# A hint for one branch, given to four engines at the head of the program

## The chip, the cores and the metric

The kernel runs on one core of one Trainium2 chip. The metric is the device time of one execution in microseconds, from start to end on the chip, as the median over several runs. Five engines work from instruction streams of their own: TensorE (PE in the profile, with PEld for its weight loads), VectorE (DVE), ScalarE (ACT), GpSimd (POOL) and SyncE (SP), which here only starts DMAs and waits for semaphores. A q behind an engine's name (SPq) stands for its sequencer.

## What is computed

Three parts follow each other, in float32 on inputs of which some are stored as float64:

```python
# attention: batch 4, 8 heads, 768 steps, head size 48
for t in range(S):
    state = alpha[:, :, t, :, None] * state + einsum('bhd,bhe->bhde', k[:, :, t], v[:, :, t])
    y[:, :, t] = einsum('bhd,bhde->bhe', q[:, :, t], state)
# first feed-forward part: xk, xr mix each row of x with the row before it
k = maximum(xk @ w_k, 0.0)
x = 1 / (1 + exp(-(xr @ w_r))) * (k * k @ w_v)
# second: a convolution over three rows as a gate
h = maximum(x @ w_in, 0.0)
out = (h * sigmoid(conv3(h, conv_w))) @ w_out
```

## The kernel before, in words

The attention's recurrence is computed in chunks of 128 steps (24 in all) with matrix products, which is exact enough only while alpha stays between 0.75 and 1.25 and the float64 words stay in range. The feed-forward parts run on tiles of 256 rows, with each float32 factor split into a high and a low part, so that three matmuls stand for one. All of this is recorded first as a list of operations (`pl`), which a planner (`Plan`) puts into an order for each engine from its own table of costs; `pl.issue` (line 1096) then issues them. The change does not touch the planner or its input.

While it works, the kernel collects in a tile `odd` by how much any input is out of range. `in_range` (line 993) counts at the end in how many of the 128 partitions all is in range, through one DVE reduction, one small matmul and a cast into `odd_i`. Line 1097 loads that count from SBUF into a register of every engine (`values_load`, TENSOR_LOAD in the trace). Line 1098 then branches: with a count below 128, `step_by_step` (line 976) computes everything again in the slow way, step by step, in loops. With the inputs here the count is 128, so every engine jumps over that part, which is long in the programs of SP, PE, DVE and ACT. Behind the jump stand the instructions that bring the semaphores to the same values on both paths (they carry line 1098 in the trace: eight on SP, one on each of the others), and the end of the program, in which SP waits for all queues and engines, and all engines meet (line 1126, the launch).

```python
        n_even = nc.values_load(odd_i, min_val=0, max_val=P)
    with tc.If(n_even < P):
        step_by_step()
```

Of the kernel before, what the change touches and what calls it, by code (L numbers as in the profile page):

```python
# [442 lines left out]
def gated_scan_ffn_kernel(  # L443
# [20 lines left out]
    P = 128  # L464
# [63 lines left out]
    odd = cp.tile([P, NCH + 40], F32, name="odd")  # L528
# [56 lines left out]
    def narrow(dst, words, col=None):  # L585
        h, l = words[..., 1], words[..., 0]
        bits = dst.bitcast(I32)
        pl.vector.tensor_scalar(even(bits), even(h), 3, 0x3FFFFFFF, op0=ALU.logical_shift_left, op1=ALU.bitwise_and)
        pl.vector.scalar_tensor_tensor(bits, h, -0x40000000, bits, op0=ALU.bitwise_and, op1=ALU.bitwise_or)
        pl.vector.scalar_tensor_tensor(bits, l, 29, bits, op0=ALU.logical_shift_right, op1=ALU.bitwise_or)  # L590
        h = h.bitcast(F32)
        pl.scalar.activation(h, h, AF.Abs)
        if col is None:
            pl.vector.scalar_tensor_tensor(dst, h, least, dst, op0=ALU.is_ge, op1=ALU.mult)
        else:
            pl.scalar.activation(h, h, AF.Relu, scale=-1.0, bias=least_s, accum_out=odd[:, col:col + 1])

    def pieces(w):

        nr = ND if w.shape[0] == DM else 2  # L600
        n = RAW // nr
        return [(slice(r, r + nr), slice(c, min(c + n, w.shape[1])))
                for c in range(0, w.shape[1], n) for r in range(0, w.shape[0] // P, nr)]

    def weight(w, hi, lo, at, src, col, whole=None):
        r, c = at
        nr, n = r.stop - r.start, c.stop - c.start
        words = src.take(pl, I32)[:, 0:2 * nr * n]
        pl.sync.dma_start(words.rearrange("p (r n) -> p r n", r=nr),
                          w[r.start * P:r.stop * P, c].bitcast(I32).rearrange("(r p) n -> p r n", p=P))  # L610
        x = whole[:, r, c] if whole else cols(v2(temps.take(pl))[:, 0:nr * n], n)
        narrow(x, words.rearrange("p (r n t) -> p r n t", r=nr, t=2), col)
        if not whole:
            split(hi[:, r, c], lo[:, r, c], x)
# [148 lines left out]
    def advance(c):  # L763
        qc, vc = qd[c % 2], vt[c % 2]
        ps = [cols(scs.take(pl)[:, 0:ND * HC], HC) for _ in range(2)]


        work, last = [[] for _ in range(4)], [[] for _ in range(4)]
        for dt in range(ND):
            for quad in range(4):  # L770
                p, i = divmod(dt * 4 + quad, 3)
                for j in range(2):
                    h = slice(HC * j, HC * j + HC)
                    for hp in range(max(0, i - 1), min(2, i + 1)):
                        work[quad].append((j, dt, vc[h, p, 32 * (i + hp):32 * (i + hp) + 32], am[h, p, hp, :]))
                    if j or not first(c):
                        last[quad].append((j, dt, ub[j][:, p, 32 * i:32 * i + 32], qc[:, p, h]))
        order = [(quad, *w[n]) for lists in (work, last) for n in range(max(map(len, lists)))
                 for quad, w in enumerate(lists) if n < len(w)]


        start = {x[:2]: n for n, x in reversed(list(enumerate(order)))}
        stop = {x[:2]: n for n, x in enumerate(order)}
        with pl.group():
            for n, (quad, h, dt, x, y) in enumerate(order):
                pl.tensor.matmul(ps[h][32 * quad:32 * quad + 32, dt, :], x, y,
                                 start=n == start[quad, h], stop=n == stop[quad, h])
        j = c % 2
        if j == 0:
            if first(c):  # L790
                pl.gpsimd.memset(xt[:, :, 0:1], 0.0)
            else:
                pl.scalar.activation(xt[:, :, 0:1], xt[:, :, T:T + 1], AF.Copy)
        for h in range(2):
            t0 = 1 + C * j + HC * h
            pl.scalar.activation(xt[:, :, t0:t0 + HC], ps[h], AF.Copy)
# [204 lines left out]
    with tc.manual_schedule():  # L1001
        nc.vector.memset(ones, 1.0)
        make_identity(nc, ident)
        for y, eng in (((sa, sk, sq), nc.vector), *((x, pl.gpsimd) for x in early.values())):
            for x, fill in zip(y, (1.0, 0.0, 0.0)):
                eng.memset(cols(v2(x), 64)[:, 0:H, D:], fill)
        nc.vector.memset(ad, 0.0)
        nc.vector.memset(odd, 0.0)
        for x in kks.pool.tiles:
            nc.vector.memset(x[:, 0:NP * D], 0.0)  # L1010
        nc.vector.memset(least_s, least)
        nc.scalar.activation(odd1, ones[:, 0:1], AF.Sigmoid)
        for x in vt:
            nc.gpsimd.memset(x[:, :, D:80], 0.0)
        nc.gpsimd.memset(one_l, 0.0)
        nc.gpsimd.memset(v3(one_l)[:, :, C - 1:C], 1.0)
        nc.gpsimd.memset(rec_f, 0.0)
        mf = tmps.tiles[0]
        make_upper_triangular(nc, mf[:, :P])
        for i in range(2):  # L1020
            h = slice(HC * i, HC * i + HC)
            nc.vector.tensor_copy(mask[h], mf[h, h])
        for x in (am, *ub):
            nc.gpsimd.memset(x, 0.0)

        cw_raw = cp.tile([P, 3, NF, 2], I32, name="cw_raw")
        prep(0)
        col = NCH
        lent = Line(Pool([v2(ht)[:, 0:2 * RAW].bitcast(I32)]))
        for x, whole in zip(weights, (None, wrw, wvw, None, None)):  # L1030
            for y in pieces(x[0]):
                i = col - NCH
                weight(*x, y, lent if i < NLENT and i % 3 == 2 else raws, col, whole)
                col += 1
        for r in lent.roots:
            pl.seen.setdefault(ht.tensor.name, []).extend((True, 0, 4, -1, o) for o in r.ops)
        for x, y, z in ((mu_ks, nu_ks, mu_k), (mu_rs, nu_rs, mu_r)):
            pl.sync.dma_start(x, z.rearrange("(a p) -> p a", p=P))
            pl.vector.tensor_scalar(y, x, -1.0, 1.0, op0=ALU.mult, op1=ALU.add)
        for i in range(3):  # L1040
            pl.sync.dma_start(cw_raw[:, i], conv_w[i].bitcast(I32).rearrange("(f p t) -> p f t", p=P, t=2))
        narrow(cw, cw_raw)

        prep(1)

        def att(n):

            attend(n)
            advance(n)
            if n + 2 < NCH:  # L1050
                prep(n + 2)

        def early_k():
            return stage_k(mix(mu_ks, nu_ks, True), True), stage_r(mix(mu_rs, nu_rs, False, True))

        att(0)
        att(1)
        y = early_k()
        att(2)
        att(3)  # L1060
        x0 = stage_v(*y, True)
        y = early_k()
        settle(*weights[1], wrw)
        att(4)
        x1 = stage_v(*y, True)
        settle(*weights[2], wvw)
        big = stage_h(0, x0)
        att(5)
        stage_o(0, big, 0, True)
        xk = mix(mu_ks, nu_ks)  # L1070
        big = stage_h(1, x1)
        xr = mix(mu_rs, nu_rs)
        stage_o(1, big, 0, True)
        for u in range(2, NU):
            c0 = 2 * u + 2
            more = u + 1 < NU
            big = stage_k(xk)
            g = stage_r(xr)
            if more:
                attend(c0)  # L1080
            x = stage_v(big, g)
            if more:
                advance(c0)
                if c0 + 2 < NCH:
                    prep(c0 + 2)
            big = stage_h(u, x)
            if more:
                att(c0 + 1)
                xk = mix(mu_ks, nu_ks)
                xr = mix(mu_rs, nu_rs)  # L1090
            else:
                stage_last(T * NU - 1)
            stage_o(u, big)
        in_range()
        warm = lambda x: nc.tensor.matmul(x[0:64, 0:64], ones, ones, start=True, stop=True)
        pl.issue(600.0, 6, banks.pool, 30e3, warm)
        n_even = nc.values_load(odd_i, min_val=0, max_val=P)
    with tc.If(n_even < P):
        step_by_step()


# [31 lines left out]
```

## Time and profile before

| what | value |
|---|---|
| median of 3 runs | 591.57 us (589.94 to 591.70) |
| the profiled execution | 591.75 us, of which the span of its instructions is 590.0 us |
| PE busy | 561.5 us, 95% of the span |
| DVE, ACT, POOL busy | 497.2, 434.6, 13.3 us |
| last matmul issued for the output | near 579.8 us into the span |
| last write of the output started | 580.7 us |

All times in the profile count from the span's first instruction. Register, branch and semaphore instructions are not counted as busy, so the last 9 us of the span look empty in the views of busy time; the view of one source line shows them, with the time at which each started (to 0.1 us). Instructions reach an engine by DMA as well: queue q8 and queue q14 carry packets of kind "instruction".

### The profile page before, as it was taken

Reading aid. Unit: us, or ns where it says so; the run is one execution under the profiler, and the core shown is the slowest. Engines: PE = TensorE matmul, PEld = TensorE weight load, DVE = VectorE, ACT = ScalarE, POOL = GpSimd, SP = SyncE. Lnnn points to the kernel's source line nnn. Section 1 sums busy time; section 2 is a strip of 40 time slices with the busy share of each in tenths; the row PEclk is TensorE's granted clock in tenths of the full one; section 3 lists DMA queues with packets and bytes.
Section 4 is the critical chain, followed back from the end, with each engine's and each line's share of the span. In section 5 each row is a group of like instructions: output and inputs, shape, how many; then the busy total and the mean of one; then the engine's idle time right before and its main releaser. Section 6 shows DMA issues by size and latency. Waiting matters only on the chain.

```text
span 590.0 us, 18574 instructions
## 1 busy us (share of the span) xinstructions
PE 561.5 (95%) x7762; PEld 527.0 (89%) x7762; DVE 497.2 (84%) x1044; ACT 434.6 (74%) x1035; POOL 13.3 (2%) x61
## 2 busy tenths in 40 slices
PE   8689899999899999999999999999999999999993
PEld 7578788999789999998999999999999999999982
DVE  8998999999999989789789789789789788376280
ACT  3799998997669577677678677677678677587370
POOL 3000000000000000000000000000000000000000
PEclk9789999999979999999999999999999999999997
DMA  9988946003433323223223223223223111000000
GB/s 182 235 168 240 233 147 186 16 28 102 107 81 83 84 65 90 52 65 92 50 65 91 59 58 92 50 64 92 50 65 91 27 41 42 1 2 29 0 2 33
DMA packets 87408, 48.02 MB, mean 81 GB/s; under 512 B 49170, under 2 KB 81810, under 8 KB 87314
## 3 DMA queue, kind: packets, MB, share of 16 engines
q1 hardware_dynamic: 87314, 46.74, 32.4%
q8 instruction: 62, 1.02, 0.7%
q14 instruction: 32, 0.26, 0.1%
HBM read 42.00 MB, written 4.72 MB: 79 GB/s over the span
## 4 chain that ended last, share of the span: by engine, by line
PE 59%; DVE 26%; ACT 9%; issue 2%; DMA 1%; SPq 1%; POOL 1%; DVEq 0%; POOLq 0%; ACTq 0%
PE pf L297 49%; DVE tmp L297 8%; PE sc L297 7%; DVE x L297 4%; DVE qd L297 3%; PE kk L297 3%; ACT tmp L297 3%; DVE gt L297 2%; DVE bigl L297 2%; ACT raw L297 1%; ACT ht L297 1%; DMA sa<-in_alpha_dram 1%; DVE kd L297 1%; ACT bigh L297 1%; DVE bt L297 1%
## 5 line engine op out<-in xcount | busy, mean ns | idle before, releaser
L297 PE MATMUL pf<-bigh,wv 128*128 128x256 f32 x336 | 88.9, 308 | 1.6 <-DVE kd L297 1.6
L297 DVE SCALAR_TENSOR_TENSOR tmp<-ht,cw,tmp 128x256 f32<-128x256 f32 x192 | 86.3, 477 | 4.7 <-ACT tmp L297 4.2
L297 ACT ACTIVATE tmp<-tmp 128x256 f32<-128x256 f32 (+1 forms) x144 | 69.2, 485 | 25.4 <-DVE tmp L297 11.6
L297 PE MATMUL pf<-xh,wih 128*128 128x256 f32 x288 | 82.0, 286 | 2.6 <-ACT xh L297 1.5
L297 PE MATMUL pf<-xl,wih 128*128 128x256 f32 x288 | 81.2, 282 | 1.4 <-DVE xl L297 1.4
L297 PE MATMUL pf<-xl,wkh 128*128 128x256 f32 x288 | 81.0, 283 | 0.5 <-DVE xl L297 0.5
L297 PE MATMUL pf<-xh,wkh 128*128 128x256 f32 x288 | 79.1, 281 | 1.9 <-ACT xh L297 1.6
L297 PE MATMUL pf<-xh,wil 128*128 128x256 f32 x288 | 80.8, 281 | 0.0
L297 PE MATMUL pf<-xh,wkl 128*128 128x256 f32 x288 | 80.0, 280 | 0.0
L297 PE MATMUL pf<-bigh,wvh 128*128 128x256 f32 x240 | 68.3, 285 | 0.3 <-DVE bigl L297 0.3
L297 PE MATMUL pf<-bigl,wvh 128*128 128x256 f32 x240 | 66.8, 278 | 0.0
L297 PEld LDWEIGHTS pf<-bigh,wv 128*128 128x128 f32 x336 | 62.8, 188 | 4.4 <-DVE kd L297 2.0
L297 PE MATMUL pf<-woh,bigh 128*128 128x384 f32 x192 | 66.4, 347 | 0.1
L297 PE MATMUL pf<-woh,bigl 128*128 128x384 f32 x192 | 64.7, 345 | 0.0
L297 PE MATMUL pf<-wol,bigh 128*128 128x384 f32 x192 | 64.4, 339 | 0.0
L297 ACT ACTIVATE pf<-pf 128x512 f32<-128x512 f32 x88 | 51.1, 583 | 11.6 <-PE pf L297 10.1
L297 PEld LDWEIGHTS pf<-xh,wih 128*128 128x128 f32 x288 | 55.3, 192 | 3.9 <-ACT xh L297 1.8
L297 PEld LDWEIGHTS pf<-xl,wih 128*128 128x128 f32 x288 | 55.3, 192 | 1.9 <-DVE xl L297 1.9
L297 PEld LDWEIGHTS pf<-xh,wkh 128*128 128x128 f32 x288 | 54.3, 190 | 2.5 <-ACT xh L297 2.1
L297 PEld LDWEIGHTS pf<-xl,wkh 128*128 128x128 f32 x288 | 54.9, 191 | 1.3 <-DVE xl L297 0.9
L297 PEld LDWEIGHTS pf<-xh,wil 128*128 128x128 f32 x288 | 55.3, 192 | 0.0
L297 PEld LDWEIGHTS pf<-xh,wkl 128*128 128x128 f32 x288 | 55.1, 191 | 0.0
(164 smaller groups left out, 1393.3 us busy)
## 6 DMA issues: line engine op xcount, KB each, us to landing
vt<-in_v_dram SPq DMA_DIRECT2D x48, 96.0 KB, 3.1
out_dram<-ot SPq DMA_DIRECT2D x23, 192.0 KB, 2.0
sa<-in_alpha_dram SPq DMA_DIRECT2D x38, 96.0 KB, 2.2
sk<-in_k_dram SPq DMA_DIRECT2D x38, 96.0 KB, 2.4
sq<-in_q_dram SPq DMA_DIRECT2D x38, 96.0 KB, 2.3
raw<-in_moe_w_out_dram SPq DMA_DIRECT2D x4, 768.0 KB, 4.4
sa<-in_alpha_dram SPq DMA_DIRECT2D x38, 80.0 KB, 2.2
sk<-in_k_dram SPq DMA_DIRECT2D x38, 80.0 KB, 2.6
```

Of the source, the lines that this page charges most:

```text
L297: getattr(getattr(self.nc, x.eng), fn)(*args, **kw)
```

## The change

Two lines: the `If` gets a label, and a hint that the branch with that label is likely to be taken is asked for on PE, SP, DVE and ACT. POOL gets none.

```diff
         pl.issue(600.0, 6, banks.pool, 30e3, warm)
+
+        tc.mark_branch_hint_location("odd", "LikelyTaken", [getattr(mybir.EngineType, e) for e in ("PE", "SP", "DVE", "Activation")])
         n_even = nc.values_load(odd_i, min_val=0, max_val=P)
-    with tc.If(n_even < P):
+    with tc.If(n_even < P, label="odd"):
         step_by_step()
```

The call stands behind `pl.issue`, yet the hint lands at the head of each of the four programs. Here is SP's program against the one before, at its head and at the branch (tiles: `sa`, `sk` are loads of alpha and k, `ot` the rows of the output, `raw` a weight of the step-by-step path; ISA stands for register work and a range check on the loaded count).

```order
@@ -1,3 +1,4 @@
-L1126 UNCONDITIONAL_BRANCH
+L1128 UNCONDITIONAL_BRANCH
+L1128 BRANCH_PREFETCH_HINT
 L297 DMA sa<-in_alpha_dram 128x8x48
 L297 DMA sk<-in_k_dram 128x8x48
@@ -208,7 +209,7 @@
 L297 DMA out_dram<-ot_84 128x384
 L297 DMA out_dram<-ot_83 128x384
-L1097 TENSOR_LOAD odd_i
-L1097 ISA x2
-L1098 COMPARE_AND_BRANCH
+L1099 TENSOR_LOAD odd_i
+L1099 ISA x2
+L1100 COMPARE_AND_BRANCH
```

One instruction is added ahead of SP's first DMA; at the branch nothing is added or moved, only the line numbers differ by two. ACT's program shows the same at its head (`odd` and `ones` are small tiles):

```order
@@ -1,3 +1,4 @@
-L1126 UNCONDITIONAL_BRANCH
+L1128 UNCONDITIONAL_BRANCH
+L1128 BRANCH_PREFETCH_HINT
 L1012 ACT_TABLE_LOAD
 L1012 ACTIVATE odd_102<-ones 128x1
```

DVE and PE get the same one row each, POOL none. The built programs differ in one more thing that the diff does not name: the label to which line 1098 jumps is now marked to begin a block of instruction fetch, on all five engines. In the program before it has no such mark, while the heads of the loops inside `step_by_step`, whose closing branches carry hints already, do have it.

## Rows read from the trace of the kernel before

**Rows 1.** The page's head, and busy us by engine (share of the span).
```profile
span 590.0 us, 18574 instructions
PE 561.5 (95%) x7762; PEld 527.0 (89%) x7762; DVE 497.2 (84%) x1044; ACT 434.6 (74%) x1035; POOL 13.3 (2%) x61
```

**Rows 2.** Busy time by stretch, 580 to 590 us: PE, PEld, DVE, ACT, POOL, clock, DMA, GB/s.
```profile
580.00:581.00 1.00, 0.22 (x3) 0.09 (x2) 0.14 (x1) 0.49 (x1) 0.00 (x0) 1.00 0.53 192
581.00:582.00 1.00, 0.00 (x0) 0.00 (x0) 0.00 (x0) 0.00 (x0) 0.00 (x0) 1.00 0.48 172
...
584.00:585.00 1.00, 0.00 (x0) 0.00 (x0) 0.00 (x0) 0.00 (x0) 0.00 (x0) 0.50 0.00 0
...
589.00:590.00 1.00, 0.00 (x0) 0.00 (x0) 0.00 (x0) 0.00 (x0) 0.00 (x0) 0.50 0.00 0
```

**Rows 3.** Source line 1098, all engines: duration ns min/median/max, first and last start us.
```profile
L1098 SPq EVENT_SEMAPHORE  x8: 17/17/17, 585.5 to 588.6; - x8
L1098 ACTq COMPARE_BRANCH  x1: 50/50/50, 581.0 to 581.0; - x1
L1098 POOLq COMPARE_BRANCH  x1: 45/45/45, 581.1 to 581.1; - x1
L1098 DVEq COMPARE_BRANCH  x1: 72/72/72, 581.1 to 581.1; - x1
L1098 PEldq COMPARE_BRANCH  x1: 3548/3548/3548, 581.1 to 581.1; - x1
L1098 POOLq EVENT_SEMAPHORE  x1: 17/17/17, 581.5 to 581.5; - x1
L1098 SPq COMPARE_BRANCH  x1: 45/45/45, 581.9 to 581.9; - x1
L1098 PEldq EVENT_SEMAPHORE  x1: 51/51/51, 584.7 to 584.7; - x1
L1098 ACTq EVENT_SEMAPHORE  x1: 17/17/17, 585.0 to 585.0; - x1
L1098 DVEq EVENT_SEMAPHORE  x1: 21/21/21, 585.3 to 585.3; - x1
```

**Rows 4.** Waits of SP's queue: waited for, us in total, times, longest.
```profile
SPq L1098 <- SPq L1098: 6.1, 2, 3.6
```

**Rows 5.** Source line 1098 on SP, 584 to 587 us, then 587 to 589 us.
```profile
L1098 SPq EVENT_SEMAPHORE  x2: 17/17/17, 585.5 to 585.6; - x2
...
L1098 SPq EVENT_SEMAPHORE  x6: 17/17/17, 588.2 to 588.6; - x6
```

**Rows 6.** DMA by queue, 582.6 to 583.4 us, then 586.0 to 586.8 us.
```profile
DMA packets 1, 0.01 MB, mean 10 GB/s; under 512 B 0, under 2 KB 0, under 8 KB 0
...
q14 instruction: 1, 0.01, 4.1%
...
q14 instruction: 1, 0.01, 2.4%
```

**Rows 7.** The last write: SP's timeline from 580 us; DMA issues, 580 to 590 us.
```profile
580.70 0.33 SPq L297 DMA_DIRECT2D out_dram<-ot  x1
...
out_dram<-ot SPq DMA_DIRECT2D x1, 192.0 KB, 2.3
```

**Rows 8.** Source line 1126, the end of the program, on SP and on DVE.
```profile
L1126 SPq EVENT_SEMAPHORE  x10: 17/28/28, 588.7 to 589.9; - x10
...
L1126 DVEq DRAIN  x2: 10/14/17, 585.4 to 589.5; - x2
```

**Rows 9.** Source line 1115, the program's first instructions, on SP.
```profile
L1115 SPq MOVE  x4: 29/34/42, 0.0 to 0.2; - x4
```

**Rows 10.** DMA by queue, 0 to 14 us, then 14 to 26 us.
```profile
DMA packets 9624, 2.53 MB, mean 181 GB/s; under 512 B 9240, under 2 KB 9240, under 8 KB 9624
q1 hardware_dynamic: 9624, 2.53, 113.5%
...
q8 instruction: 3, 0.05, 1.9%
```

**Rows 11.** Busy time by stretch at the head, columns as in rows 2.
```profile
14.00:28.00 14.00, 8.53 (x243) 6.92 (x243) 13.04 (x26) 9.37 (x19) 0.00 (x0) 0.82 1.03 223
```

## The prediction

> **What bounds the kernel now.** Over the span as a whole PE does: it is busy for 95% of 590.0 us [rows 1]. The hint gives PE no less to multiply, so I looked for a stretch in which PE is not the limit and a branch is. The busy time by stretch shows it at once: the last engine work falls between 580 and 581 us, and from there to 590.0 us no engine is busy at all [rows 2]. These last 9 us hold only loads of the count, branches and semaphores, which that view does not count, so the next view is that of the branch's own source line [rows 3]. Read it per engine, from COMPARE_BRANCH to the EVENT_SEMAPHORE behind the jump. POOL: 581.1 to 581.5, 0.4 us. PE: the branch itself is recorded with 3548 ns. ACT: 581.0 to 585.0, 4.0 us. DVE: 581.1 to 585.3, 4.2 us. SP, which branches last because it had a write to start first: 581.9 to 585.5, 3.6 us. All five take the same jump; only POOL, whose program over the skipped path is short, arrives without a stall.
>
> SP then stalls a second time. Of its eight instructions behind the jump, two run at 585.5 and 585.6, and the other six from 588.2 to 588.6 [rows 5]. The list of SP's waits has both gaps in one row: 6.1 us in 2 waits, the longest 3.6, so the other is 2.5 [rows 4]. It names no engine and no data that SP waited for. What does move in these gaps is instructions: during the first, one packet of the instruction queue q14 between 582.6 and 583.4 us; during the second, one between 586.0 and 586.8 us [rows 6]. I read the first gap as the fetch of the block that holds the jump's target, and the second as the fetch of the next block, which is needed two instructions later because the target stands two short of a block's end. Everything behind is SP's: it starts its last waits at 588.7 us [rows 8], while DVE, the last of the others, had been through at 585.4 us [rows 8]. So **SP's two fetch stalls set the end.**
>
> The Trainium skill, in "Runtime: NRT & Kernel Launch", section "Instruction fetch mechanics", says that a jump to a target outside of the blocks that an engine holds must wait for a DMA of that block; the rows above agree, with 3.6 to 4.2 us on the three engines whose gap can be read.
>
> **The change, part by part.**
>
> *The hint instructions.* One each on SP, DVE, ACT and PE, at the head. No trace here has one. From below it costs nothing, where the engine waits for data anyway; from above I take SP's register moves, 29 to 42 ns [rows 9], and the longest of the branches without a fetch in it, 72 ns [rows 3]. SP's loads and DVE's first fills stand right behind it, so I count 0.05 us on the path, with ends 0 and 0.1.
>
> *The first stall.* If the block of the target is there when SP branches, the jump costs what POOL's does, 0.4 us, instead of 3.6: SP arrives at 582.3 us rather than 585.5, a gain of 3.2 us. From below the hint may save nothing (the block is not there), from above the whole 3.6. I take POOL's, the same instruction at the same place.
>
> *The second stall.* The mark that the label has now asks that the target begin a block. Then SP's eight instructions and the end of its program would stand in one block, and the 2.5 us wait falls away. No trace here shows what becomes of such a mark, so its worth lies between 0 and 2.5 us. I take 2.5: the target is two instructions short of the border, so little needs to be moved, and the mark is what the program's other hinted targets carry.
>
> *What is late next.* SP's third instruction behind the jump waits for the queue that carries the last write of the output. That write is issued at 580.7 us and lands 2.3 us later, at 583.0 us [rows 7]. SP would be there at 582.5 us (582.3 and two instructions, 0.1 us apart as in [rows 5]), so it now waits some 0.5 us for the write. From that third instruction to the end it takes 590.0 - 588.2 = 1.8 us [rows 1, 5], all semaphores and the meeting of the engines, which nothing shortens. So the span ends near 583.0 + 1.8 = 584.8 us.
>
> *The other engines.* With their hints PE, ACT and DVE arrive near 581.5 us, 0.4 us behind their branches [rows 3], and wait for SP. Were only DVE to keep its stall, the end would be set by its 585.4 us [rows 8] and at most the 1.3 us that SP's last waits and the meeting of the engines take from 588.7 to 590.0: 586.7 us, a gain of 3.3 instead of 5.2.
>
> **The sum.** 590.0 - 584.8 = 5.2 us less, 0.05 more at the head: about 5.1 us. The profiled execution took 591.75 us, 0.18 above the median of 591.57; its own time would become 586.65, and the median **586.5 us**, 0.9% faster. About 0.3% (1.8 us) is what a measurement of this kernel can tell from no change; the three runs of before lie within that.
>
> **The rivals.**
>
> *Only the first stall goes* (the mark moves nothing, or SP's next block is still late). SP arrives at 582.3, stalls for 2.5 us after two instructions as now, and goes on at 585.0, 3.2 us earlier than the 588.2 of today; the write has landed by then. Time: 591.57 - 3.2 = 588.4 us. For it speaks that the packet of the second gap is only fetched once SP has arrived, some 1 us behind 585.5 [rows 5, 6]; against it, that the target's place is not left as it was.
>
> *The fetch runs straight on, whatever the hint says,* or the hint, given 580 us ahead of its branch, is forgotten by then. SP then still pays 3.6 us at the jump. If the mark is heeded, the second stall goes all the same: 591.57 - 2.5 = 589.1 us. If it is not, the change does nothing it says: 591.6 us. For this speaks that between the hint and the branch every engine goes through many blocks, and no row shows that anything is kept that long. The same page and section of the Trainium skill say that the fetch ahead is purely sequential; by that rule it would be 589.1 or 591.6 us, and no run here shows yet whether a hint is an exception to it.
>
> *Slower: the target's block is fetched at once, at the head,* and takes the place of the next block in line. In the first 14 us no instruction packet moves at all [rows 10]: the engines run there from what they hold. Thrown out of order, an engine would find its second block missing and stall for as long as PE does at the jump, 3.5 us [rows 3]. PE's fetches begin between 14 and 26 us [rows 10], a stretch in which DVE is busy for 13.04 of 14 us [rows 11], so that a stall of DVE there has no cover. Nothing is gained at the end, as the block is long gone by then: 591.57 + 3.5 = 595.1 us. It decides if the fetch follows the hint itself and not the approach of the branch. Against it: the loops of the skipped path use the same instruction with a branch further on.
>
> **How the numbers follow.** Both stalls gone, 586.5 us: 0.55. Only the first gone (or one engine's hint lost): 0.17, 588.4. Only the second: 0.11, 589.1. Neither: 0.10, 591.6. Slower: 0.07, 595.1. The first three together are 0.83, and the range covers them with half of the spread of the runs shown (0.9 us) at either end: 586.5 - 0.9 = 585.6 to 589.1 + 0.9 = 590.0 us. Faster by over 0.3% means below 589.8: nearly all of the first two and some two thirds of the third, 0.78; the rest of the third and the case without effect make 0.15 within 0.3%; slower 0.07.
>
> **What the profile of the changed kernel would show.** At the branch's line, SP's EVENT_SEMAPHORE would start 0.4 us behind its COMPARE_BRANCH, ACT's and DVE's as well, and PE's branch would lose its 3548 ns. The eight on SP would run without a gap of 2.5 us, with one of some 0.5 us ahead of the third, and the row of SP's waits on itself would shrink from 6.1 us to under 1. Packets for the targets would move ahead of 581 us. The forecast is wrong if any of the three gaps of 3.6 to 4.2 us is still there, if the six late semaphores still come 2.5 us behind the first two, or if instruction packets turn up in the first 14 us. PE's busy time should stay at 561.5 us.

## The result and the profile after

The changed kernel takes 587.45 us (median of 8 runs, 586.25 to 588.19) against 591.86 us for the kernel before in the same comparison. The ratio is 0.9917, with a 95% interval of 0.990 to 0.9934: faster by 3.9 to 5.9 us, where 5.1 were forecast, with a median of 586.5 us in a range of 585.6 to 590.0. The profiled execution took 586.33 us, with a span of 584.4 us; forecast were 584.8.

The page's head and busy times, for [rows 1]:

```profile
span 584.4 us, 18578 instructions
...
PE 564.0 (97%) x7762; PEld 529.5 (91%) x7762; DVE 496.4 (85%) x1044; ACT 434.4 (74%) x1035; POOL 13.8 (2%) x61
```

The four additional instructions are the hints. The counted instructions of every engine are the same in number. PE's 2.5 us more did not lengthen anything, as the cast of the count, DVE's last work, starts at nearly the same time before and after:

```profile
580.25 0.14 DVE L297 CAST odd_i<-kk 1x1 int32<-1x1 f32 x1 [4.88 <-PE kk L297]
580.31 0.15 DVE L297 CAST odd_i<-kk 1x1 int32<-1x1 f32 x1 [4.81 <-PE kk L297]
```

So in these two profiles the whole difference lies behind that point: 9.7 us from the cast to the end of the span before, 4.1 us now. The branch's source line, now 1100, answers to [rows 3]:

```profile
L1100 SPq EVENT_SEMAPHORE  x8: 17/17/17, 582.5 to 583.1; - x8
L1100 ACTq COMPARE_BRANCH  x1: 68/68/68, 581.1 to 581.1; - x1
L1100 POOLq COMPARE_BRANCH  x1: 45/45/45, 581.1 to 581.1; - x1
L1100 DVEq COMPARE_BRANCH  x1: 84/84/84, 581.1 to 581.1; - x1
L1100 PEldq COMPARE_BRANCH  x1: 497/497/497, 581.2 to 581.2; - x1
L1100 ACTq EVENT_SEMAPHORE  x1: 17/17/17, 581.6 to 581.6; - x1
L1100 POOLq EVENT_SEMAPHORE  x1: 17/17/17, 581.6 to 581.6; - x1
L1100 PEldq EVENT_SEMAPHORE  x1: 51/51/51, 581.7 to 581.7; - x1
L1100 DVEq EVENT_SEMAPHORE  x1: 21/21/21, 581.8 to 581.8; - x1
L1100 SPq COMPARE_BRANCH  x1: 70/70/70, 582.0 to 582.0; - x1
```

From branch to arrival it is now 0.5 to 0.7 us by these rows on every hinted engine, as on POOL, which has no hint; before it was 3.6 to 4.2. SP's eight instructions run from 582.5 to 583.1 without a gap, where two and six of them stood 2.6 us apart [rows 5]. SP's waits on itself, of the same line, for [rows 4]:

```profile
SPq L1100 <- SPq L1100: 0.5, 1, 0.5
```

One wait of 0.5 us is left of two with 6.1, and it is the jump itself. The hints, and SP's instructions of the program's last line:

```profile
L1128 SPq EVENT_SEMAPHORE  x10: 17/28/28, 583.1 to 584.4; - x10
...
L1128 ACTq BRANCH_PREFETCH_HINT  x1: 45/45/45, 0.7 to 0.7; - x1
L1128 SPq BRANCH_PREFETCH_HINT  x1: 51/51/51, 0.7 to 0.7; - x1
L1128 DVEq BRANCH_PREFETCH_HINT  x1: 51/51/51, 0.8 to 0.8; - x1
L1128 PEldq BRANCH_PREFETCH_HINT  x1: 50/50/50, 0.8 to 0.8; - x1
```

Where did the target's block come from? The DMA view from 575 to 577.5 us shows, for the kernel before and then for the changed one, which queues moved packets:

```profile
DMA packets 2, 0.00 MB, mean 1 GB/s; under 512 B 1, under 2 KB 2, under 8 KB 2
...
q1 hardware_dynamic: 2, 0.00, 0.2%
```

```profile
DMA packets 3, 0.02 MB, mean 7 GB/s; under 512 B 1, under 2 KB 2, under 8 KB 2
...
q8 instruction: 1, 0.02, 2.8%
```

A packet of instructions is new here, on q8, whose 62 packets only PE with its 7762 matmuls and as many weight loads can need, some 5 us ahead of PE's branch and 575 us behind its hint. By itself it does not show the target's block. Run one below, in which PE has no hint, moves such a packet from 575 to 577.5 us as well, the 63rd on its page where the others count 62, and PE's branch takes 3643 ns there all the same:

```profile
q8 instruction: 1, 0.02, 2.4%
```

What goes with the hint is the packet right behind the branch. From 581.9 to 582.45 us q8 moves one before, and one in run one, but none in the changed kernel. Before:

```profile
q8 instruction: 1, 0.02, 12.3%
```

So the block that PE had to fetch at its jump was already there. That the packet of 576 us brought it fits the times, but is not shown. In the first 14 us there is still no instruction packet (all 9472 packets belong to the data queue):

```profile
DMA packets 9472, 2.50 MB, mean 179 GB/s; under 512 B 9088, under 2 KB 9088, under 8 KB 9472
...
q1 hardware_dynamic: 9472, 2.50, 111.5%
```

### The profile page after: what moved, and what is told of

It reads as the page before. It is cut to its first block, busy times and chain, and to the rows that moved or that the text cites. A ratio compares the mean times of both kernels' runs of the same rounds, so it can differ in the third digit from the quotient of the medians.

```text
span 584.4 us, 18578 instructions
## 1 busy us (share of the span) xinstructions
PE 564.0 (97%) x7762; PEld 529.5 (91%) x7762; DVE 496.4 (85%) x1044; ACT 434.4 (74%) x1035; POOL 13.8 (2%) x61
## 4 chain that ended last, share of the span: by engine, by line
PE 64%; DVE 20%; ACT 9%; DMA 2%; issue 2%; SPq 1%; POOL 0%; DVEq 0%; ACTq 0%; POOLq 0%
PE pf L297 54%; PE sc L297 6%; DVE tmp L297 6%; DVE x L297 3%; PE kk L297 3%; ACT tmp L297 3%; DVE qd L297 2%; DVE gt L297 2%; ACT raw L297 2%; DVE bigl L297 1%; ACT ht L297 1%; SPq L297 1%; DMA sq<-in_q_dram 1%; DVE kd L297 1%; DMA raw<-in_moe_w_v_dram 1%
```

## The experiments

Theory A is the prediction's: the hint brings the block of its own engine's target ahead of the jump, the mark that comes with it frees SP of the second stall, and whichever engine arrives last sets the end. The rivals B to G are named in the expectations. Each kernel was timed against the kernel before. Line numbers of the branch and of the program's end vary with the edits.

**One: the hint on SP alone.**

```diff
-        tc.mark_branch_hint_location("odd", "LikelyTaken", [getattr(mybir.EngineType, e) for e in ("PE", "SP", "DVE", "Activation")])
+        tc.mark_branch_hint_location("odd", "LikelyTaken", [getattr(mybir.EngineType, e) for e in ("SP",)])
```

> The hint is given to SP alone; the jump's target keeps its mark on all engines. Theory A (each engine's own hint brings the block of its own target, and the end is set by whichever engine comes last): SP arrives 0.5 us behind its branch as in the changed kernel, but DVE, ACT and PE stall again for 4.2, 4.0 and 3.5 us; DVE arrives at 585.3 us and some 1.0 us of SP's last waits and the meeting of the engines follow: span near 586.4 us, 3.6 us below before, ratio 0.994. Rival B (SP's hint is all that counts): span 584.4 us, ratio 0.991.

Measured: span 586.0 us, ratio 0.9947 (0.9927 to 0.9967). The branch's line, without POOL and ACT, and then SP's longest wait behind it:

```profile
L1100 SPq EVENT_SEMAPHORE  x8: 17/17/17, 582.4 to 583.2; - x8
...
L1100 DVEq COMPARE_BRANCH  x1: 72/72/72, 581.1 to 581.1; - x1
L1100 PEldq COMPARE_BRANCH  x1: 3643/3643/3643, 581.1 to 581.1; - x1
...
L1100 DVEq EVENT_SEMAPHORE  x1: 21/21/21, 585.0 to 585.0; - x1
```

```profile
SPq L1128 <- DVEq L1100: 1.4, 1, 1.4
```

SP arrives early and then waits 1.4 us for DVE, which has its stall, of 3.9 us here. Rival B falls on the trace: an engine without the hint keeps its stall, and it sets the end once SP does not. The two ratios themselves are too close to be told apart.

**Two and three: the hint on all but SP, and on POOL alone.** The same line, with `("PE", "DVE", "Activation")`, and with `("Pool",)`.

> The hint is given to PE, DVE and ACT, not to SP. Theory A: SP pays 3.6 us at its jump and arrives at 585.5 us; the mark on the target alone removes its second stall, and from its arrival to the end it takes 1.9 us as in the changed kernel: span near 587.4 us, 2.6 us below before, ratio 0.9957. Rival C (a mark without the hint of the same engine moves nothing): both of SP's stalls stay, span 590.0 us, ratio 1.0. Rival B, as far as the others' hints are worth nothing: 587.4 or 590.0 as well.

> The hint is given to POOL alone, which has no stall at its jump; so the four others have the mark on the target and no hint. Theory A: SP, DVE, ACT and PE stall for 3.6, 4.2, 4.0 and 3.5 us at the jump, SP has no second stall: span near 587.4 us, 2.6 us below before, ratio 0.9957, as with the hint on all but SP. Rival C: 590.0 us, ratio 1.0.

Measured: spans 587.3 and 587.7 us, ratios 0.9971 (0.9955 to 0.9987) and 0.9979 (0.9967 to 0.9991). SP's wait on itself in run two, then in run three:

```profile
SPq L1100 <- SPq L1100: 3.7, 1, 3.7
```

```profile
SPq L1100 <- SPq L1100: 3.4, 1, 3.4
```

One wait each, where the kernel before has two [rows 4]: the mark works on an engine that has no hint itself, and rival C falls. In run three ACT, DVE and PE pay their stalls in full and the end moves by only 0.4 us, behind a cast that is 0.75 us later (580.71 against 579.96 us): as long as SP is late, the other hints are worth nothing here.

**Four: no hint and no mark, the target moved.** In the kernel before, at the end of `step_by_step`:

```diff
             stage_last(b * S + S - 1)
+        for _ in range(4):
+            nc.sync.dma_start(outf[0:1, 0:64], ones[0:1, 0:64])
```

> The kernel before, without hint and mark, with four small DMAs added on SP at the end of the step-by-step path, which is jumped over: they never run, and only move the jump's target some five instructions further on SP. Theory A (the second stall comes from the target standing two instructions short of a block's end): the target then stands a few instructions behind the border, SP stalls 3.6 us at the jump and not a second time: span near 587.4 us, ratio 0.9957. Rival D (the second stall has another cause, such as a wait for the last write): both gaps stay, span 590.0 us, ratio 1.0.

Measured: span 587.5 us, ratio 0.9965 (0.9951 to 0.9979).

```profile
L1100 SPq EVENT_SEMAPHORE  x8: 17/17/17, 585.5 to 586.1; - x8
```

```profile
SPq L1100 <- SPq L1100: 3.6, 1, 3.6
```

The second stall is gone here too, through four instructions that never run. It was a matter of where the target stands, and rival D falls.

**Five and six: the hint, with the target moved.** In the changed kernel, the same loop with `range(108)`, and with `range(60)`.

> The changed kernel (hint on four engines, mark on the target) with 108 small DMAs added on SP at the end of the skipped path, which never run: they put the jump's target some 19 or 20 instructions short of the end of a fetch block, where the mark, as far as I know, leaves it. Of the 21 instructions from the target to the program's end the last few then stand in the next block. Theory A with its second half (the hint brings one block, and the next is asked for only on arrival, to be there some 2.6 us later): SP arrives 0.5 us behind its branch, runs some 19 instructions to 583.8 us, and waits until near 585.1 us: span near 585.6 us, 1.2 above the changed kernel. Rival E (the hint brings the next block too, or the mark moves the target even from there): no gap, span 584.4 us.

> As in the run before, with 60 DMAs in place of 108: the target now stands in the middle of a fetch block on SP, far from either border, so that the mark has nothing to do and the whole end of the program lies in the target's block. Theory A: span 584.4 us as in the changed kernel, ratio 0.991, so that with the hint the mark is worth something only where a border is near. Rival F (a target must begin its block for the hint to bring it): SP stalls 3.6 us again, span 587.4 us.

Measured: spans 585.2 and 583.7 us, ratios 0.9928 (0.9904 to 0.9953) and 0.9917 (0.9892 to 0.9943). In run five, SP's waits on itself at the program's end, now line 1130, and the one instruction of that line that SP runs from 584 us on:

```profile
SPq L1130 <- SPq L1130: 1.3, 1, 1.3
```

```profile
L1130 SPq EVENT_SEMAPHORE  x1: 17/17/17, 585.2 to 585.2; - x1
```

SP stalls for 1.3 us ahead of its very last instruction, 2.7 us behind its arrival at 582.5: the next block is not brought along, and is there 2.6 to 2.7 us after arrival as in [rows 5]. That was A's number; the span is 0.4 us under it since only one instruction was left to run. Rival E falls. In run six SP's part of the branch's line is this:

```profile
L1102 SPq EVENT_SEMAPHORE  x8: 17/17/17, 581.8 to 582.4; - x8
```

Nothing stalls, and from the cast (579.60 us) to the end it is 4.1 us, the changed kernel's number. A target in mid-block is served as well as one at a border, and rival F falls.

**Seven: the branch laid out the other way round,** without a hint:

```diff
-    with tc.If(n_even < P):
+    with tc.If(n_even < P, preferred_fallthrough_block=False):
```

> The kernel before, without a hint, with the branch laid out the other way round: the path that is taken here follows the branch directly, and the jump over the step-by-step path stands behind the semaphore instructions instead of ahead of them. Theory A (every jump to a block that is not there costs 3.4 to 4.2 us, wherever it stands): SP runs its eight instructions from 582.1 us, waits for the last write until 583.0, jumps near 583.4, arrives some 3.5 us later, near 587.0, and needs 1.3 us from there: span near 588.3 us, 1.7 below before, ratio 0.997; a border within its last 13 instructions would add up to 2.5. Rival G (a jump without a condition is foreseen, or no jump is left): span near 584.8 us.

Measured: span 588.6 us, ratio 0.9958 (0.9942 to 0.9974). SP's part of the branch's line, then of the program's end:

```profile
L1098 SPq EVENT_SEMAPHORE  x8: 17/17/17, 583.5 to 584.3; - x8
L1098 SPq COMPARE_BRANCH  x2: 43/46/49, 583.4 to 584.4; - x2
```

```profile
L1126 SPq EVENT_SEMAPHORE  x10: 17/28/28, 587.3 to 588.5; - x10
```

The first branch is not taken, and SP goes on 0.1 us later; the second is an unconditional jump at 584.4 us, and SP arrives at 587.3, 2.9 us later. Rival G falls. The layout hides the wait for the write ahead of the jump but keeps a stall, so it gains less than the hint. Its price at the jump is 2.9 us where 3.5 were expected; the span came out near the expected one only because the cast was 1.4 us later (581.63 us), which is luck.

No version beat the changed kernel by more than can be measured.

## Why the prediction held

*What bounds.* Right. The end of the span was set by SP's two stalls; with both gone the stretch from cast to end shrank by 5.6 us. The timed gain has this within its interval of 3.9 to 5.9.

*The first stall* was priced at a gain of 3.2 us with POOL's 0.4 for the jump. SP's jump took 0.5 (its own wait row), so it was 3.1. Runs two and three bring the stall back on SP alone or on all.

*The second stall* was taken at its upper end, 2.5 us, on the strength of a mark in the built program. Shown by runs two and three with the mark and by run four with neither. This was the boldest choice, as no trace then showed what a mark does: had it been idle, 588.4 us would have come out.

*What is late next* was right in kind and mis-sized. SP was to wait some 0.5 us for the last write, up to 583.0 us; it arrived 0.2 us later than forecast (582.5 instead of 582.3) and did not wait at all, as the write landed earlier. The DMA view from 580 us, and the start of the write:

```profile
out_dram<-ot SPq DMA_DIRECT2D x1, 192.0 KB, 1.9
```

```profile
580.76 0.33 SPq L297 DMA_DIRECT2D out_dram<-ot  x1
```

It took 1.9 us to land where it had taken 2.3 [rows 7], so the end is set by SP's own jump and its 21 instructions: 582.5 + 1.9 = 584.4 us instead of 583.0 + 1.8 = 584.8. Where the write lands later, SP does wait for it. In run one it took 2.2 us, and SP has a second wait of 0.3 us beside the 0.5 of its jump:

```profile
SPq L1100 <- SPq L1100: 0.8, 2, 0.5
```

The write took 2.1 to 2.3 us before and in runs one, three and four, in which the packet that PE fetches at its jump starts while the write is landing. It took 1.9 us in the changed kernel and in runs two, five and six, in which PE fetches none at its jump, and in run seven, in which that packet starts after the landing. This division fits a delay by that fetch; no run varied it by itself.

*The other engines.* Right that they must not stall either: run one shows DVE as the next in line, with a span of 586.0 us where 586.7 was the bound given.

*The head.* 0.05 us was counted, with 0.1 as the upper end; the hint on SP took 51 ns, and SP's first load started at 0.85 us instead of 0.75, so it was 0.1 there. Whether any of it reaches the end is not shown: the cast starts anywhere from 579.60 us (run six) to 581.63 (run seven), and the 0.06 us between the two profiles is far below that.

*The rivals.* That the fetch only runs straight on, and that a hint is forgotten over 580 us, fell with the jumps of 0.5 us: on SP in run one with its own hint alone, against a wait of 3.7 in run two without it. The rule of the Trainium skill ("Runtime: NRT & Kernel Launch", "Instruction fetch mechanics") that fetching ahead is purely sequential agrees in these runs with the stalls of SP, PE, DVE and ACT where they have no hint (2.9 to 4.3 us from branch to arrival), and not with their jumps of 0.5 to 0.7 us where they have one: here the measurement decides. That the fetch happens at the head fell with the first 14 us, in which no instruction packet moves.

## What to carry to other kernels

Look at the time between the last counted work and the end of the span, line by line and engine by engine: a jump over a path that is long in an engine's program cost 2.9 to 4.3 us in these runs, and a block border just behind its target cost SP 2.5 us more. A hint takes the first away on the engines that carry it, and the place of the target decides the second; both pay only on the engine that arrives last, until another takes its place. A change of layout that merely moves the jump keeps most of its price (2.9 of 3.6 us in run seven).

## What the runs showed that was not expected

On two engines the stall is a little shorter with the mark and no hint: from branch to arrival DVE took 3.9 us and ACT 3.7 to 3.8 in runs one and three, against 4.2 to 4.3 and 4.0 without the mark, before and in run four. SP's and PE's do not follow: SP waited 3.7 us (run two) and 3.4 (run three) with the mark and 3.6 without it, and PE's branch took 3643 and 3568 ns (runs one and three) with it and 3548 and 3588 without. Why was not tested.

The page counts 28 packets on q14 in the changed kernel where it was 32. One of the four is SP's second block: runs three and four, without a second stall and without a hint on SP, DVE or ACT, count 31. The others follow the hints: 30 with SP's alone (run one), 29 with DVE's and ACT's (run two), 28 with all three. Up to 580.3 us q14 moves 24 in every run, so those that are missing are the ones fetched at the jumps. That the targets' blocks came in place of blocks straight ahead among the 24 fits the count, but no run shows which packet is which.
